# Fill constants of q and k written in eight transfers and later, large convolution constants loaded later, splits in another order

## The chip, the cores and the metric

The kernel runs on one core of a Trainium2 chip. What is measured is device time in microseconds from launch to the last output. A time is the median of several runs; a profile is one execution with the hardware's recorder on. The core has five engines with instruction streams of their own: TensorE (PE, matmuls, with its weight loads as PEld), VectorE (DVE), ScalarE (ACT), GpSimd (POOL) and SyncE (SP), which here issues nearly all transfers. Every engine works through its stream in order and stops at an instruction whose semaphores have not come yet. Sixteen DMA engines carry out the transfers.

## The reference

Two independent parts are computed and set side by side in the output. The first is attention over a window of 256 positions, with 32 heads of width 18, with its projections before and after. The second is a state-space convolution: a kernel K of length 2048 for each of 576 channels, computed from A, B, C and dt, and applied to u by a Fourier transform of twice the length.

```python
def _A_ref(x, wqkv, wo):                 # x [1, 2048, 576]
    qkv = (x @ wqkv).reshape(B, S, 3, H, Dh).transpose(2, 0, 3, 1, 4)
    q, k, v = qkv[0], qkv[1], qkv[2]     # H = 32, Dh = 18
    scores = jnp.einsum("bhqd,bhkd->bhqk", q, k) * (Dh ** -0.5)
    mask = (idx[:, None] - idx[None, :] >= 0) & (idx[:, None] - idx[None, :] < 256)
    p = softmax(jnp.where(mask, scores, -1e9))
    return (p @ v).transpose(0, 2, 1, 3).reshape(B, S, D) @ wo

def _B_ref(u, A_re, A_im, B_re, B_im, C_re, C_im, log_dt, Dskip):
    dt = jnp.exp(log_dt)[:, None]        # D = 576 channels, N = 128 states
    P = jnp.exp((dt * A)[:, :, None] * l[None, None, :])
    K = jnp.einsum("dn,dnl,dn->dl", Cc, P, dt * Bc).real
    y = irfft(rfft(pad(u)) * rfft(pad(K)))[:L]
    return y + u * Dskip

return jnp.concatenate([a, b], axis=-1)
```

## The kernel before

The two parts are cut into small steps and woven into one another. Each kind of step is a stream, written as a generator: the projection of q, k and v (`proj`), the tables of exponentials and sines of the convolution (`g_fac` to `g_taps`), the scores and their maxima (`smax`, `scores`), the products with v (`pv`), the transforms of the convolution (`cload`, `cspec`, `cinv`, `hload`, `clast`) and some more. Nothing is scheduled by the machine: four strings (`PLAN`) name one after the other the stream that takes its next step, for the parts "front", "tables", "first" and "rest". A digit behind a letter takes the oldest posted follow-up of that stream, such as the copy out of PSUM or the store of what was copied. So the order of instructions on each engine, and of transfers on SP, is the order of the strings.

SP's transfers go through one hardware queue, and each waits until the eighth transfer before it has landed. So at most eight are in flight, and they share the DMA engines in the order of their issue.

The projection works through the 2048 tokens in four quarters c (512 tokens each). For each quarter x is split into a high and a low 16-bit half (`xconv`, lines 376 to 387): ACT makes the high half `xh`, for each half h of the quarter; DVE makes the rest `xl` of rows 0 to 511 (line 384, long) and a low half of the last 64 rows, which goes into the fifth block of `xh` (line 386, short). Each product on PE then is a sum of fourteen matmuls (line 205), whose fifth reads that block. Nine products give q and k; ACT (line 451) and DVE (line 454) copy their high and low halves to a tile `qst` (three buffers), and SP stores them (lines 467 and 468) to the DRAM arrays `qz` and `kz`, of shape [4 quarters, 8 groups, 64 rows, 4, 512] in 16 bits. Four more give v, for which ACT's copies (line 443) go to four tiles `vst0` to `vst3` and SP's stores to `vd` (line 472). The first quarter's v is made apart, by `vfirst`.

Rows 0 to 53 of `qz` and `kz` are what is stored; rows 54 to 63 are constant, -32768. They are written from a constant tile `ones` in two transfers at the end of `vfirst` (lines 412 to 414), one for `qz`, one for `kz`, in the front. Row 54 is overwritten later in SBUF with the maxima of the scores (`raw<-m`, line 935, four small transfers for each of the 16 items of attention). An item is one quarter of the queries with eight heads; its q, k and v are loaded by `parts` (lines 880 to 884).

Meanwhile the tables of the convolution's kernel are made (lines 506 to 660): taps go from PSUM to a tile `kst` (line 649 on DVE, two buffers) and with two transfers to `gk` (line 641). Tiles `ust` with the first transform of u go to `gx` (line 496). In the part "rest", `conv_load` loads from both an `xk` of each of 24 steps (line 708), `spectra` (line 720) multiplies it with the constants `w2`, and `inverse` (line 754) the product with `i1`. Both constants, [128, 8, 256] in 32 bits, and a small one `i2` are loaded by `conv_setup` at the start of this part (line 778). The constants of the masks and maxima (`idb`, `sm`, `tm`, `idf`) are loaded by `early` (line 840).

Of the kernel before, what the change touches and what calls it, by code (L numbers as in the profile page):

```python
# [11 lines left out]
F16 = mybir.dt.float16  # L12
# [3 lines left out]
OP = mybir.AluOpType  # L16
# [5 lines left out]
CQ = 512  # L22
# [20 lines left out]
def constants():  # L43
# [23 lines left out]
    for nm, v in mult.items():  # L67
# [16 lines left out]

PLAN = {
    "front":
        "AAACVAAAVCAAAVAAV1V1VCACVVV1AAAAVCAV1VCVV1CVCCCCAPV1CVCBBCBVACAV1V1VVCPCBPPPP1CP2P4PPPP1CP2P4PBCBPPP"
        "1P",
    "tables":
        "GG1GG5PG6GP1P2P2GPG5G6GG2NG1G2G5G6GPPPPPP4P4G5G6P1P2MM1P4MMM1MNP1GG1RP2PNPPPP4RRG2GGP1GG5P2PG6G5G6NG"  # L90
        "1MM1XX1NRG2RPMUUU1U2UUUU2XMRPM1U1MP1P2PP4X1PXX5GGG5X2G6P1MG5RRG6PXX1XGM1MNX1MRG1G2M1NP2PPXX2PPU4X5RR"
# [64 lines left out]
class Kernel:  # L156
# [219 lines left out]
    def xconv(self, c):  # L376
        nc = self.nc
        self.xh = xh = self.p["xx"].tile([128, 5, 512], F16, name="xh")
        self.xl = xl = self.p["xx"].tile([128, 4, 512], F16, name="xl")
        for hf in range(2):  # L380
            t = self.xt[2 * c + hf]
            h = xh[:, :, hf * 256:hf * 256 + 256]
            nc.scalar.activation(h, t, AF.Copy, scale=self.sx)
            nc.vector.scalar_tensor_tensor(xl[:, :, hf * 256:hf * 256 + 256], t[:, 0:4], self.sx, h[:, 0:4],
                                           op0=OP.mult, op1=OP.subtract)
            nc.vector.scalar_tensor_tensor(h[64:128, 4], t[64:128, 4], self.sx[64:128], h[64:128, 4],
                                           op0=OP.mult, op1=OP.subtract)

    def vfirst(self):
        nc, w = self.nc, self.wt  # L390
        for tk in range(4):
            v, x = self.vst[tk], self.xt[tk // 2]
            ts = slice(tk % 2 * 128, tk % 2 * 128 + 128)
            ps = []
            for hf in range(2):
                yield "PE", (w, x), "pp"
                ps.append(self.p["pp"].tile([128, 512], F32, name="pp")[:, :288])
                for k in range(4):
                    nc.tensor.matmul(ps[hf], x[:, k, ts], w[:, k, 1152 + 288 * hf:1440 + 288 * hf],
                                     start=(k == 0), stop=False)  # L400
            yield "PE", ()
            for hf in range(2):
                r = slice(64 * hf, 64 * hf + 64)
                nc.tensor.matmul(ps[hf], x[r, 4, ts], w[r, 4, 1152 + 288 * hf:1440 + 288 * hf], start=False, stop=True)
            for hf in range(2):
                self.post("1", (ps[hf],), lambda v=v, hf=hf, x=ps[hf]: nc.scalar.activation(  # L406
                    v[:, 16 * hf:16 * hf + 16, 0:18], x.rearrange("p (h d) -> p h d", d=18), AF.Copy))
        yield "SP", (), lambda: self.known and not self.pend.get("V1")
        for tk in range(4):
            self.v_store(0, tk, self.vst[tk])  # L410
        yield "SP", ()
        for z in (self.qz, self.kz):
            nc.sync.dma_start(z[:, :, 54:64].rearrange("c g r p n -> (c g) r (p n)"),
                              self.ones[0:32].unsqueeze(1).to_broadcast([32, 10, 4 * CQ]))

    def proj(self):
        nc, w = self.nc, (self.wh, self.wl)
# [24 lines left out]
    def v_evac(self, c, tk, v, hf, x):  # L442
        self.nc.scalar.activation(v[:, 16 * hf:16 * hf + 16, 0:18], x.rearrange("p (h d) -> p h d", d=18), AF.Copy,
                                  scale=self.vsc)
        if hf:
            self.post("6", (v,), lambda: self.v_store(c, tk, v))

    def qk_hi(self, c, m, ps):
        nc, S = self.nc, 2.0 ** -24
# [253 lines left out]
    def conv_load(self, n):  # L703
        nc, fs, (ch, t) = self.nc, self.p["fs"], divmod(n, 8)
        x = self.cl[n] = fs.tile([128, 4, 2, 192], F32, name="xk")
        for m, g in enumerate((self.gx, self.gk)):
            yield "SP", ()
            nc.sync.dma_start(x[:, :, m], g[8 * t:8 * t + 8, :, :, 192 * ch:192 * ch + 192]
                              .rearrange("(s r) a l j -> (r a l) s j", r=2))

    def spectra(self, n):
        nc, tt, fy, t = self.nc, self.nc.vector.tensor_tensor, self.p["fy"], n % 8
# [58 lines left out]
    def conv_setup(self):  # L771
        nc, a, cc = self.nc, self.a, self.p["cc"]
        self.cl, self.Y, self.hp = {}, {}, {}
        self.i2 = cc.tile([128, 64], F32, name="i2")
        self.w2 = cc.tile([128, 8, 256], F32, name="w2")
        self.i1 = cc.tile([128, 8, 256], F32, name="i1")
        for n in ("w2", "i1", "i2"):
            nc.sync.dma_start(getattr(self, n), a["c_" + n])

    def cload(self):  # L780
        for n in range(24):
# [50 lines left out]
    def early(self):  # L832
        nc, a, ap = self.nc, self.a, self.p["const"]
        yield "SP", ()
        self.idb = ap.tile([128, 64], BF, name="idb")
        self.sm = ap.tile([128, 128], BF, name="sm")
        self.tm = ap.tile([128, 640], BF, name="tm")
        self.idf = ap.tile([128, 128], F32, name="idf")
        for t, n in ((self.idb, "c_id"), (self.sm, "c_sm"), (self.tm, "c_tm"), (self.idf, "c_if")):
            nc.sync.dma_start(t, a[n])  # L840
        for i in range(2):
            yield "SP", ()
            raw = {z: self.p["rawp"].tile([128, 5, 256], F32, name="raw").rearrange("p a b -> p (a b)") for z in "QKV"}
            q, k = (raw[z].bitcast(F16)[:, 0:4 * CQ].rearrange("p (a n) -> p a n", a=4) for z in "QK")
            self.sets[i].update({"Q": q, "V": raw["V"][:, 0:928]})
            self.first[i].update({"Q": q, "V": raw["V"][:, 0:928], "K": Shifted(k, 256), "k": k, "old": raw["K"]})
            nc.gpsimd.memset(raw["V"][:, 912:928], 0.0)
            for n, part in enumerate(self.parts(i)):
                if n:
                    yield "SP", ()  # L850
                part()
# [301 lines left out]
    def build(self):  # L1153
        nc, a = self.nc, self.a
        with ExitStack() as es:
# [28 lines left out]
            self.wh = self.p["wq"].tile([128, 5, 1728], F16, name="wh")  # L1184
            self.wl = self.p["wq"].tile([128, 5, 1728], F16, name="wl")
            self.vst = [self.p["pj"].tile([128, 32, 19], F32, name="vst%d" % i) for i in range(4)]
            self.ones = self.p["wrp"].tile([128, 4 * CQ], F16, name="ones")
            nc.gpsimd.memset(self.ones, -32768.0)
            self.known, self.conv_n = False, 0
            self.xh = self.xl = None  # L1190
# [84 lines left out]
```

## Time and profile before

| | |
|---|---|
| Median of 3 runs | 777.15 us (776.16 to 780.92) |
| The profiled execution's own time | 772.85 us |
| Its span | 771.1 us |
| Mean granted clock of PE | 0.98 |
| The two fills of `qz` and `kz` | 1280 KB each |
| Loads of `w2` and of `i1` | 1024 KB each |
| A store of `kst` | 256 KB |
| Bytes moved over the span | 150.67 MB, 195 GB/s in the mean |

The span is the time between the first and the last instruction that the recorder saw; the execution's own time is 1.75 us longer. The profiled execution was 4.3 us faster than the median. In all views, times count from the start of the span, and a name stands for all buffers of a tile: `w` is `w2`, `i` is `i1` or `i2`, `raw` is any buffer of a pool that serves in turn x, q, k and v.

### The profile page before, as it was taken

The page shows a single profiled execution, that of the slowest core. Times are in us where ns is not written, and L with a number is a line of the kernel's source. Part 1 is how long each engine was busy: PE and PEld are TensorE (multiplying, and loading weights), DVE is VectorE, ACT ScalarE, POOL GpSimd, SP SyncE. Part 2 cuts the span into 40 slices and gives each one's busy share as a digit, 9 for nine tenths or more (in the row PEclk, how much of TensorE's full clock was granted, in tenths as well). Part 3 has the DMA queues.
Part 4 walks back from the last instruction along what each step waited for, and adds up shares of the span by engine and source line. Part 5 has one row for each costly group of instructions (what it writes and reads, how often), then busy time and mean ns, then how long its engine had stood idle before and what let it go on. Part 6 is the DMA issues. An engine that isn't in the chain of part 4 may idle for free.

```text
span 771.1 us, 29480 instructions
## 1 busy us (share of the span) xinstructions
PE 686.8 (89%) x12956; PEld 403.5 (52%) x12956; DVE 538.7 (70%) x689; ACT 548.3 (71%) x755; POOL 415.8 (54%) x309
## 2 busy tenths in 40 slices
PE   3768768999999989999888998989899989999997
PEld 2523334556655655566445545545554545576675
DVE  5884888677787677888859877988886788631200
ACT  2267986888988878895467686677687687766722
POOL 2242886888788696867016553544255355354420
PEclk9978999999999999999989999999999999999999
DMA  8996342863657686757967667586588766767875
GB/s 308 345 248 151 86 109 56 196 156 97 133 146 201 145 195 188 178 150 155 244 213 236 201 186 246 176 273 183 177 246 233 231 206 191 230 189 250 251 237 174
DMA packets 215904, 150.67 MB, mean 195 GB/s; under 512 B 103530, under 2 KB 195818, under 8 KB 215520
## 3 DMA queue, kind: packets, MB, share of 16 engines
q1 hardware_dynamic: 214160, 146.28, 67.0%
q0 software_dynamic: 1616, 2.52, 1.1%
q8 instruction: 101, 1.65, 0.9%
q14 instruction: 27, 0.22, 0.1%
HBM read 83.50 MB, written 65.11 MB: 193 GB/s over the span
## 4 chain that ended last, share of the span: by engine, by line
PE 53%; DVE 12%; ACT 12%; issue 4%; DMA 4%; SPq 2%; POOL 0%; ACTq 0%; DVEq 0%
PE pp L205 9%; PE po L1022 9%; PE ring L205 7%; DVE m L942 5%; PE ring L908 4%; PE ring L754 4%; PE ring L984 4%; PE ring L720 3%; PE ring L617 2%; PE ring L817 2%; PE ring L494 2%; ACT P L1002 2%; PE ring L506 2%; DMA K<-kz 2%; PE ring L633 1%
## 5 line engine op out<-in xcount | busy, mean ns | idle before, releaser
L942 DVE TENSOR_REDUCE m<-ring 128x2 f32<-128x640 f32 (+4 forms) x256 | 188.3, 778 | 42.4 <-PE ring L916 37.1
L588 POOL TENSOR_TENSOR m<-A,tr 128x1024 f32<-128x1024 f32 x72 | 142.0, 1991 | 43.1 <-DVE m L594 37.1
L1002 ACT ACTIVATE P<-ring,esc 128x1024 f32<-128x1024 f32 (+2 forms) x86 | 88.4, 1060 | 28.7 <-PE ring L997 28.0
L1002 ACT ACTIVATE raw<-ring,esc 128x1024 f32<-128x1024 f32 (+2 forms) x74 | 76.9, 1061 | 28.6 <-PE ring L997 26.7
L736 POOL TENSOR_TENSOR t<-X 128x768 f32<-128x768 f32 x24 | 45.9, 1913 | 79.7 <-ACT X L728 79.5
L1065 POOL TENSOR_TENSOR oh<-osb,oh 128x1024 f16<-128x1024 f32 x16 | 35.4, 2211 | 66.2 <-ACT oh L1061 63.3
L205 PE MATMUL pp<-xh,wh 128*128 128x512 f16 x180 | 47.3, 393 | 14.5 <-ACT vst L406 6.4
L205 PEld LDWEIGHTS <-wh 128*128 128x128 f16 x324 | 31.2, 100 | 49.6 <-issue 10.5
L916 PE MATMUL ring<-sm,idb 64*64 64x128 bf16 x896 | 52.8, 219 | 0.0
L603 DVE TENSOR_TENSOR Q<-fr,ring 128x1024 f32<-128x1024 f32 x36 | 43.8, 1216 | 11.6 <-ACT ring L527 11.3
L728 ACT ACTIVATE X<-ring 128x768 f32<-128x768 f32 x48 | 36.7, 811 | 21.2 <-PE ring L720 12.5
L594 DVE TENSOR_TENSOR m<-m,m 128x1024 f32<-128x1024 f32 x36 | 48.3, 1342 | 4.2 <-POOL m L588 4.2
L1057 POOL TENSOR_TENSOR osb<-osb,T 128x1024 f32<-128x1024 f32 x16 | 37.8, 2365 | 24.3 <-DVE T L1052 21.8
L205 PE MATMUL pp<-xh,wl 128*128 128x512 f16 x180 | 48.5, 403 | 1.5 <-DVE wl L373 1.5
L908 PE MATMUL ring<-K,raw 54*64 54x320 f16 (+4 forms) x576 | 43.3, 308 | 5.6 <-DVE m L942 1.6
L569 POOL TENSOR_TENSOR tr<-tr,mab 128x768 f32<-128x768 f32 x18 | 33.7, 1871 | 25.6 <-ACT tr L564 25.6
L908 PEld LDWEIGHTS <-raw 54*64 54x64 f16 x704 | 26.1, 104 | 39.3 <-issue 35.6
L742 POOL TENSOR_TENSOR Y<-t,t 128x384 f32<-128x384 f32 x24 | 24.0, 1000 | 39.7 <-DVE t L736 18.7
L720 PE MATMUL ring<-xk,w 64*32 64x384 f32 x768 | 41.5, 491 | 3.5 <-issue 2.8
L997 PE MATMUL ring<-tm,idb 64*64 64x256 bf16 (+2 forms) x640 | 44.6, 257 | 0.0
L984 PEld LDWEIGHTS <-K 55*64 55x64 f16 x1280 | 29.1, 106 | 27.8 <-issue 24.0
L617 PE MATMUL ring<-Q,m 128*32 128x64 f32 x2304 | 39.2, 220 | 4.1 <-DVE m L594 2.0
(170 smaller groups left out, 1668.5 us busy)
## 6 DMA issues: line engine op xcount, KB each, us to landing
gx<-ust SPq DMA_DIRECT2D x16, 576.0 KB
gk<-kst SPq DMA_DIRECT2D x36, 256.0 KB
xk<-gx SPq DMA_DIRECT2D x24, 384.0 KB
xk<-gk SPq DMA_DIRECT2D x24, 384.0 KB
h<-ho SPq DMA_DIRECT2D x48, 192.0 KB
hp<-h SPq DMA_DIRECT2D x24, 384.0 KB
K<-kz SPq DMA_DIRECT2D x14, 512.0 KB
raw<-qz SPq DMA_DIRECT2D x11, 512.0 KB
```

The lines of the kernel that those rows point to most:

```text
L205: self.nc.tensor.matmul(ps, u, v, start=(i == 0), stop=(i == len(ops) - 1))
L588: tt(m[part], A[:, ch, a0:a0 + 8].unsqueeze(3).to_broadcast(sh), tr[:, ch, part, 0:8].unsqueeze(2).to_broadcast(sh), op=OP.mult)
L594: self.nc.vector.tensor_tensor(m[0], m[0], m[1], op=OP.add)
L617: nc.tensor.matmul(kp[32 * st:32 * st + 32, j, :], m[:, ch, 32 * term:32 * term + 32], Q[:, ch, term, :], start=(term == 0), stop=(term == ...
L720: nc.tensor.matmul(pi[i][32 * b:32 * b + 32, s, :384], self.w2[64 * r:64 * r + 64, t, o:o + 32], x[64 * r:64 * r + 64, 2 * s + q].rearrang ...
L736: mul(ts[i], X[:, :, :, :192].rearrange("p i s j -> p s i j"), X[:, i, :, 192:].unsqueeze(2).to_broadcast(sh), op=OP.mult)
L908: nc.tensor.matmul(ps[z:z + 64, b, :n], d["Q"][rr, 2 * b + pp, 64 * qb:64 * qb + 64], d["K"][rr, 2 * b + pp, k0:k1], start=True, stop=Fals ...
L916: nc.tensor.matmul(out, self.idb[rr], self.sm[rr], start=False, stop=True, skip_group_check=True)
L942: self.nc.vector.tensor_reduce(out, x, axis=AX.X, op=OP.max)
L984: nc.tensor.matmul(ps[z:z + 64, b, off:off + w], d["K"][rr, 2 * b + pp, kc:kc + 64], d["Q"][rr, 2 * b + pp, q0:q0 + w], start=(k == 0), st ...
L1002: nc.scalar.activation(P[:, :, lo:hi], ps[:, :, lo:hi], AF.Exp, scale=self.esc)
L1022: nc.tensor.matmul(po[32 * p:32 * p + 32, z, q0:q0 + w], V[64 * z:64 * z + 64, kb * 76 + 19 * p:kb * 76 + 19 * p + 32], P[p % 2][64 * z:64 ...
```

## The change

It has three parts, and the string "front" loses one letter.

First, the fills. The two large transfers at the front go. A new function `fill(z)` writes the constant rows of one quarter of `qz` or `kz`, 320 KB in a transfer of shape 8 x 80 x 256, from the first 8 partitions of `ones`, which now holds 256 values in each of 32 partitions in place of 2048. For the quarters 1 to 3, `qz` is filled behind the store of the first tile of v, `kz` behind that of the second; for quarter 0 both stand in `early`, behind the four constants.

Second, `xconv`. For the quarters 1 to 3 DVE makes both short low halves first and then both long ones.

Third, `conv_setup` loads only `i2`; `w2` is loaded behind the first `xk<-gx` and `i1` behind the first `xk<-gk`.

```diff
     def xconv(self, c):
-        for hf in range(2):
-            t = self.xt[2 * c + hf]
-            h = xh[:, :, hf * 256:hf * 256 + 256]
+        hs = [(self.xt[2 * c + hf], *(z[:, :, hf * 256:hf * 256 + 256] for z in (xh, xl))) for hf in range(2)]
+        for t, h, _ in hs:
             nc.scalar.activation(h, t, AF.Copy, scale=self.sx)
-            nc.vector.scalar_tensor_tensor(xl[:, :, hf * 256:hf * 256 + 256], t[:, 0:4], self.sx, h[:, 0:4],
-                                           op0=OP.mult, op1=OP.subtract)
+
+        def low(t, h, _):
             nc.vector.scalar_tensor_tensor(h[64:128, 4], t[64:128, 4], self.sx[64:128], h[64:128, 4],
                                            op0=OP.mult, op1=OP.subtract)
+
+        def rest(t, h, l):
+            nc.vector.scalar_tensor_tensor(l, t[:, 0:4], self.sx, h[:, 0:4], op0=OP.mult, op1=OP.subtract)
+
+        a, b = hs
+        for f, x in ((low, a), (low, b), (rest, a), (rest, b)) if c else ((rest, a), (low, a), (rest, b), (low, b)):
+            f(*x)
 
     def vfirst(self):
...
-        yield "SP", ()
-        for z in (self.qz, self.kz):
-            nc.sync.dma_start(z[:, :, 54:64].rearrange("c g r p n -> (c g) r (p n)"),
-                              self.ones[0:32].unsqueeze(1).to_broadcast([32, 10, 4 * CQ]))
+
+    def fill(self, z):
+        z = z[:, 54:64].rearrange("g r p n -> g (r p n)").rearrange("g (y x) -> g y x", x=256)
+        self.nc.sync.dma_start(z, self.ones[0:8].unsqueeze(1).to_broadcast([8, 80, 256]))
...
     def v_evac(self, c, tk, v, hf, x):
...
+        def store():
+            self.v_store(c, tk, v)
+            if tk < 2:
+                self.fill((self.qz, self.kz)[tk][c])
+
         if hf:
-            self.post("6", (v,), lambda: self.v_store(c, tk, v))
+            self.post("6", (v,), store)
...
     def conv_load(self, n):
...
+            if n == 0:
+                z = ("w2", "i1")[m]
+                nc.sync.dma_start(getattr(self, z), self.a["c_" + z])
...
     def conv_setup(self):
...
-        for n in ("w2", "i1", "i2"):
-            nc.sync.dma_start(getattr(self, n), a["c_" + n])
+        nc.sync.dma_start(self.i2, a["c_i2"])
...
     def early(self):
...
+        for z in (self.qz, self.kz):
+            self.fill(z[0])
...
     def build(self):
...
-            self.ones = self.p["wrp"].tile([128, 4 * CQ], F16, name="ones")
+            self.ones = self.p["const"].tile([32, 256], F16, name="ones")
             nc.gpsimd.memset(self.ones, -32768.0)
```

In the listings of the order below, a row is a line of the kernel, the operation, output and input with their buffer numbers, and the shape; x2 is two in a row. The numbers of lines and buffers shift a little between the two kernels.

SP's transfers around the first place of the new fills, where the stores of v's second quarter end and the constants of the masks follow, before:

```order
L472 DMA vd_74<-vst0_147 64x8x76 x2
L472 DMA vd_74<-vst1_148 64x8x76 x2
L840 DMA idb_2149<-in_c_id_dram 128x64
L840 DMA sm_2150<-in_c_sm_dram 128x128
L840 DMA tm_2151<-in_c_tm_dram 128x640
L840 DMA idf_2152<-in_c_if_dram 128x128
L641 DMA gk_70<-kst_1794 128x16x32 x2
L641 DMA gk_70<-kst_2077 128x16x32 x2
```

The same place after:

```order
L483 DMA vd_74<-vst0_147 64x8x76 x2
L420 DMA qz_72<-ones_151 8x80x256
L483 DMA vd_74<-vst1_148 64x8x76 x2
L420 DMA kz_73<-ones_151 8x80x256
L853 DMA idb_2149<-in_c_id_dram 128x64
L853 DMA sm_2150<-in_c_sm_dram 128x128
L853 DMA tm_2151<-in_c_tm_dram 128x640
L853 DMA idf_2152<-in_c_if_dram 128x128
L420 DMA qz_72<-ones_151 8x80x256
L420 DMA kz_73<-ones_151 8x80x256
L652 DMA gk_70<-kst_1792 128x16x32 x2
L652 DMA gk_70<-kst_2077 128x16x32 x2
```

Four fills stand ahead of the taps' stores; the third quarter has its two between stores of v in the same way (further back on SP), and the fourth too.

SP's transfers at the start of the part "rest", where the large constants were loaded, before (`kst` and the maxima `m16` are stored, the rest is loaded):

```order
L641 DMA gk_70<-kst_4899 128x16x32 x2
L778 DMA w2_5264<-in_c_w2_dram 128x2048
L778 DMA i1_5265<-in_c_i1_dram 128x2048
L778 DMA i2_5263<-in_c_i2_dram 128x64
L935 DMA raw_3599<-m16_5101 1x16x64 x4
L880 DMA raw_2942<-qz_72 128x2048
L880 DMA K0_4730<-kz_73 128x4x512
L708 DMA xk_5269<-gx_69 128x4x192
L708 DMA xk_5269<-gk_70 128x4x192
```

The same place after:

```order
L652 DMA gk_70<-kst_4905 128x16x32 x2
L791 DMA i2_5269<-in_c_i2_dram 128x64
L950 DMA raw_3603<-m16_5107 1x16x64 x4
L895 DMA raw_2944<-qz_72 128x2048
L895 DMA K0_4736<-kz_73 128x4x512
L719 DMA xk_5273<-gx_69 128x4x192
L723 DMA w2_5270<-in_c_w2_dram 128x2048
L719 DMA xk_5273<-gk_70 128x4x192
L723 DMA i1_5271<-in_c_i1_dram 128x2048
```

The two large constants now stand behind the stores of the maxima and the loads of q and k.

DVE's operations on the second quarter of x, before:

```order
L515 TENSOR_TENSOR fr_847<-ring_836,fr_847 128x512
L384 SCALAR_TENSOR_TENSOR xl_856<-raw_123,xr_257,xh_855 128x4x256
L386 SCALAR_TENSOR_TENSOR xh_855<-raw_123,xr_257,xh_855 64x256
L384 SCALAR_TENSOR_TENSOR xl_856<-raw_125,xr_257,xh_855 128x4x256
L386 SCALAR_TENSOR_TENSOR xh_855<-raw_125,xr_257,xh_855 64x256
L603 TENSOR_TENSOR Q_936<-fr_639,ring_844 128x32x32
```

The same place after:

```order
L526 TENSOR_TENSOR fr_845<-ring_834,fr_845 128x512
L385 SCALAR_TENSOR_TENSOR xh_853<-raw_123,xr_257,xh_853 64x256
L385 SCALAR_TENSOR_TENSOR xh_853<-raw_125,xr_257,xh_853 64x256
L389 SCALAR_TENSOR_TENSOR xl_854<-raw_123,xr_257,xh_853 128x4x256
L389 SCALAR_TENSOR_TENSOR xl_854<-raw_125,xr_257,xh_853 128x4x256
L614 TENSOR_TENSOR Q_934<-fr_637,ring_842 128x32x32
```

The two short operations have moved ahead of the two long ones; what stands around them is as before.

More of the change, by code (lines that the diff above doesn't have):

```diff
@@ L86 @@
     "front":
-        "AAACVAAAVCAAAVAAV1V1VCACVVV1AAAAVCAV1VCVV1CVCCCCAPV1CVCBBCBVACAV1V1VVCPCBPPPP1CP2P4PPPP1CP2P4PBCBPPP"
-        "1P",
+        "AAACVAAAVCAAAVAAV1V1VCACVVV1AAAAVCAV1VCVV1CVCCCCAPV1CVCBBCBVACAV1V1VCPCBPPPP1CP2P4PPPP1CP2P4PBCBPPP1"
+        "P",
     "tables":
```

## The prediction

> **What bounds the kernel now.** I read the profile's page first: the span, the busy times and the engines of the chain that ended last.
>
> ```profile
> span 771.1 us, 29480 instructions
> PE 686.8 (89%) x12956; PEld 403.5 (52%) x12956; DVE 538.7 (70%) x689; ACT 548.3 (71%) x755; POOL 415.8 (54%) x309
> PE 53%; DVE 12%; ACT 12%; issue 4%; DMA 4%; SPq 2%; POOL 0%; ACTq 0%; DVEq 0%
> ```
>
> The tensor engine is busy for 89% and carries 53% of the chain; DMA and SP's queue carry 6%. No transfer bounds the kernel as a whole. But PE runs in order, so a DMA that comes late stops it, and the 84 us in which it is idle are all there is to win. I therefore went to the places that the change touches: the timelines of SP, ACT, PE and DVE there, and the busy time of the DMA engines in stretches around them. The columns of a timeline row are start, duration, engine, line, operation, output and input, count, and in brackets the idle time ahead of it with what ended it. The columns of a stretch are its ends and length, the busy time of PE, weight loads, DVE, ACT and POOL, PE's granted clock, the DMA share and GB/s.
>
> **The fills leave the front.** Two fills of 1280 KB are issued at 47.48 and 48.12; the stores of q behind them go out slowly, and ACT waits for one of them.
>
> ```profile
> 47.48 0.59 SPq L413 DMA_DIRECT2D qz<-ones  x1
> 48.12 0.58 SPq L413 DMA_DIRECT2D kz<-ones  x1
> 54.58 2.38 SPq L467 DMA_DIRECT2D qz<-qst  x1
> 57.01 2.46 SPq L468 DMA_DIRECT2D qz<-qst  x1
> 64.99 0.60 ACT L451 ACTIVATE qst<-pp 128x512 f16<-128x512 f32 x1 [3.47 <-DMA qz<-qst]
> 66.96 1.08 PE L506 MATMUL ring<-c_ct,Tim 96*128 96x512 bf16 x2 [2.83 <-DVE fr L515]
> 55.00:61.00 6.00, 6.00 (x31) 2.74 (x29) 4.98 (x4) 2.54 (x5) 2.73 (x1) 1.00 0.99 200
> ```
>
> A store takes SP some 2.4 us here, since each waits for the eighth DMA before it, and the engines are full (share 0.99) with the fills. ACT's 3.47 us become PE's 2.83 us two microseconds later. Without the fills the stores land as soon as they are issued. Gain: 2.8 (PE's wait) to 3.5 us (ACT's); I take 3.4, since the wait is ACT's and PE stands behind it. The shorter preset of the constant costs nothing: it is on POOL, ahead of all this.
>
> The last row also prices the new fills. The fills read 32 partitions, and the engines, all busy, move 200 GB/s. Stores that read all 128 partitions move nearly twice that with the same share:
>
> ```profile
> 283.00:284.00 1.00, 0.91 (x5) 0.43 (x5) 0.98 (x2) 0.77 (x3) 1.00 (x1) 1.00 1.03 376
> ```
>
> So the rate goes with the number of partitions that are read, or something that comes with it, more than with the engines. The new fill reads only partitions 0 to 7, for 320 KB. If a quarter of the partitions gives a quarter of the rate (50 GB/s), a fill takes 320 KB / 50 GB/s = T = 6.55 us, as long as an old one with four times the bytes. That is the upper end. The lower end is the old rate, 200 GB/s: T = 1.64. Between them lies a limit by the DMA engines alone: if the outer size of 8 lets only 8 of the 16 take part, each at an old fill's 12.5 GB/s, T = 3.3 us. I take 6.55, because 32 against 128 partitions already shows the rate falling with the partitions read, at a full share. The old row shows 32 partitions at half of the 376 GB/s, so a proportional fall below 32 is an estimate.
>
> [...]
>
> **Eight short fills at three places.** Four stand at 183 to 196 us (one behind each of two stores of v, two behind the constants of the maxima), two near 268 to 281, two near 348 to 356. All DMAs of SP pass through the same engines in order, so what is issued behind a fill lands T later. What counts is how long the engines idle there now, before the first instruction that waits.
>
> ```profile
> 183.28 5.71 SPq L472 DMA_DIRECT2D vd<-vst  x4
> 187.00:189.00 2.00, 2.00 (x15) 1.20 (x13) 2.00 (x3) 1.34 (x4) 1.26 (x1) 1.00 0.01 2
> 189.00:196.00 7.00, 6.31 (x116) 4.83 (x115) 6.64 (x8) 6.94 (x12) 5.36 (x3) 1.00 0.87 160
> 196.00:200.00 4.00, 3.49 (x28) 2.48 (x26) 3.18 (x5) 4.00 (x10) 2.44 (x2) 1.00 0.02 4
> 205.29 0.69 DVE L649 COPY kst<-ring 128x512 f32<-128x512 f32 x1
> 206.03 0.38 PE L506 MATMUL ring<-c_ct,Tim 96*128 96x512 bf16 x1 [0.28 <-DVE kst L649]
> ```
>
> Place 1: the copy at 205.29 needs the buffer whose two stores stand right behind the four fills. Now they are done at 196. The slack is 205.3 - 196 = 9.3 us, plus 2.0 + 0.13 x 7 = 2.9 us in which the engines idle before that, less an estimated 0.8 until the last store is seen: 11.4. The stall is 4T - 11.4 = 14.8 us at 6.55, 1.8 at 3.3, none at 1.64. Behind the copy stand the rest of DVE's program and, 0.05 us later, PE.
>
> ```profile
> 267.00:284.40 17.40, 15.81 (x176) 10.66 (x169) 10.06 (x12) 15.63 (x27) 15.60 (x14) 1.00 0.93 199
> 284.40:286.40 2.00, 1.57 (x7) 0.57 (x6) 1.94 (x3) 0.80 (x2) 1.91 (x3) 1.00 0.02 8
> 289.00:290.40 1.40, 1.40 (x7) 0.64 (x8) 1.40 (x2) 0.70 (x2) 1.29 (x1) 1.00 0.62 179
> 291.90 0.60 ACT L451 ACTIVATE qst<-pp 128x512 f16<-128x512 f32 x1 [0.34 <-PE pp L205]
> 345.00:358.00 13.00, 13.00 (x280) 9.24 (x278) 10.84 (x15) 7.45 (x14) 10.08 (x9) 1.00 0.93 188
> 358.00:361.00 3.00, 2.78 (x47) 2.05 (x48) 2.75 (x7) 1.00 (x2) 2.12 (x2) 1.00 0.09 13
> 356.59 2.74 SPq L935 DMA_DIRECT2D raw<-m  x4
> 364.00 0.42 PE L984 MATMUL ring<-raw 55*64 55x64 f16 x12
> 209.15 1.96 DMA qz<-qst
> ```
>
> Place 2: the engines idle 0.07 x 17.4 + 0.98 x 2.0 + 0.38 x 1.4 = 3.7 us before ACT's copy at 291.90, the first that needs a buffer of a store behind the fills; with 0.4 between 286.4 and 289 that is 4. Stall 2T - 4 = 9.1, 2.6 or none. Place 3: they idle 0.07 x 13 + 0.91 x 3 = 3.6 us until 361; the last store of maxima, issued at 359.33, lands near 361.3 by the chain's row, 2.7 before PE needs it at 364.00. The slack is between 3.6 and 6.3; I take 5.4, nearer the upper end, since these stores are small. Stall 2T - 5.4 = 7.7, 1.2 or none. Together 8T - 20.8 = 31.6 us at T = 6.55. SP's issue of a fill, 0.6 us as at 47.48, runs while the engines still move the one before; it adds nothing.
>
> **The splits in another order.** DVE's four operations are the same; the two short ones come first.
>
> ```profile
> 106.00 2.88 DVE L384 SCALAR_TENSOR_TENSOR xl<-raw,xr,xh 128x1024 f16<-128x1024 f32 x1
> 108.89 2.08 DVE L386 SCALAR_TENSOR_TENSOR xh<-raw,xr,xh 64x256 f16<-64x256 f32 x1
> 113.88 0.48 DVE L386 SCALAR_TENSOR_TENSOR xh<-raw,xr,xh 64x256 f16<-64x256 f32 x1
> 114.42 0.59 PE L205 MATMUL pp<-xh,wh 128*128 128x512 f16 x1 [4.32 <-DVE xh L386]
> 118.64 0.69 DVE L649 COPY kst<-ring 128x512 f32<-128x512 f32 x1 [0.76 <-PE ring L637]
> 120.60 1.10 PE L617 MATMUL ring<-Q,m 128*32 128x64 f32 x64
> 201.47 1.29 DVE L384 SCALAR_TENSOR_TENSOR xl<-raw,xr,xh 128x1024 f16<-128x1024 f32 x1 [0.56 <-ACT xh L383]
> ```
>
> In the second quarter of the tokens PE waits 4.32 us until both short ones are done, at 114.36. In the new order they are done after 106.0 + 2 x 2.1 = 110.2 at the latest, and PE's wait goes. But DVE still ends the four at 114.4, and until 120 it has only 0.76 us of idle time, ended by PE. PE's matmul at 120.60 reads a product that DVE makes after all this. So PE arrives there early and waits again: of 4.32 us about 0.5 stay (between none and 1.5; a loss of 0.8 if PE's earlier matmuls push DVE's order of waits). In the third quarter (201.47) and the fourth PE has other work; nothing.
>
> **The large constants.** Two transfers of 1024 KB stand ahead of four tiny stores of maxima.
>
> ```profile
> 376.17 2.12 SPq L778 DMA_DIRECT2D w<-in_c_w_dram  x1
> 379.39 7.95 DMA raw<-m
> 387.38 1.07 PE L984 MATMUL ring<-raw 55*64 55x64 f16 x12 [2.27 <-DMA raw<-m]
> 380.00:387.00 7.00, 4.74 (x128) 2.43 (x127) 6.17 (x10) 1.59 (x2) 0.00 (x0) 0.99 1.01 374
> 387.00:394.00 7.00, 6.27 (x111) 3.88 (x119) 2.40 (x4) 5.08 (x5) 0.00 (x0) 0.52 1.02 319
> 397.41 0.88 PE L720 MATMUL ring<-xk,w 64*32 64x384 f32 x16
> ```
>
> The second row is of the chain: the stores land 7.95 us after their issue, behind 2 MB; PE idles 2.26 of 7 us, and for the 7 us after that the granted clock is 0.52. Moved behind, the constants free the stores: 2.27 us of idle time, and up to 2 more if the clock stays up, since 6.27 us of matmuls at about half clock could take some 3. I take 4 (2.3 to 4.5). The cover: the first matmul that reads the weights is at 397.41. The queue has 2.9 MB to bring by then (q, k, x, weights), at 374 to 319 GB/s 8 to 9 us from 383: 392. It holds, by 5 us.
>
> **Sum.** 31.6 - 3.4 - 0.5 - 4.0 = +23.7 us. The profiled execution took 772.85 us, 4.3 under the median of the runs shown, so this gives 796.6 against the profile and 801 against the median; I say 798. In general the change is 8T - 28.7, zero at T = 3.6.
>
> **The rivals.** (a) The fills are limited by the number of DMA engines and not by the partitions: T = 3.3, stalls of 1.8 + 2.6 + 1.2 = 5.6 us, gains 7.9, -2.3 in all: 775 against the median, 771 against the profile; call it 773. [...] (b) The other side: the fills run at the old rate, T = 1.64. Then each fits into the idle time of its place (6.6 of 11.4, 3.3 of 4, 3.3 of 5.4 us) and only the gains are left: -7.9, 769. It decides as soon as T is below 2. For it: the places were idle by 2 to 12 us, and half of a fill's cost may be per DMA. Against it: 200 against 376 GB/s. (c) A part of the stalls is won back, as ACT and POOL run ahead while PE stands: if a third comes back, +13, 787. This lies inside my own case.
>
> **How the numbers follow.** The partition case with (c) in it has 0.70, its own range 784 to 808 (a third won back and a little more, to the upper bounds of the terms); (a) has 0.15, (b) 0.15. The predicted time is 798. The range of 8 in 10 reaches from 770, which takes in (a) and the upper half of (b), to 808. A measurement here tells about 1% (7.8 us) from no change: below 769.4, above 784.9. Slower by over 1% is my case less its low end, 0.66; within 1% is (a) and parts of both neighbours, 0.20; faster by over 1% is half of (b) and a little, 0.14.
>
> **What would show it.** If I am right, the stretches behind a fill have a DMA share near one (or half, for eight engines) at some 50 GB/s for 6 us, DVE's copy of the taps near 205 waits some 15 us for a store, ACT's copy of q near 290 waits for one, PE near 364 waits for the maxima. At the front the 3.47 us of ACT are gone, at 387 the 7.95 us of the chain and the low clock. I am wrong if the fills move over 100 GB/s, if those three waits are under 3 us together, or if the stores behind a fill overtake it on engines that it leaves free.

## The result, and the profile after

The changed kernel takes 812.55 us in the median (810.44 to 814.20, 4 runs) against 778.05 us before: 1.0439 times as long, with an interval of 1.0396 to 1.0481. The forecast was 798 with a range up to 808. The sign and the main cause were right. The amount was not: 34.5 us were lost, not the 23.7 of the sum.

The page of the changed kernel, its span, the busy times of the engines and the engines of the chain that ended last:

```profile
span 811.2 us, 29484 instructions
PE 697.6 (86%) x12956; PEld 408.0 (50%) x12956; DVE 539.1 (66%) x689; ACT 548.5 (68%) x755; POOL 411.3 (51%) x309
PE 51%; ACT 14%; DVE 12%; DMA 10%; SPq 6%; issue 5%; ACTq 0%; POOL 0%; DVEq 0%
```

DMA and SP's queue now have 16% of the chain where they had 6%. PE does the same 12956 matmuls, but at a mean granted clock of 0.956 in place of 0.98 it is busy for 10.8 us longer, and it is idle for 29 us longer (811.2 - 697.6 against 771.1 - 686.8). The profiled execution before was 5 us faster than its median, so the profiles differ by 40 us where the medians differ by 34.5.

The first place of the new fills, in the timelines of SP, DVE and PE, and the busy times in four stretches of 1 us (columns as in the prediction):

```profile
184.38 0.49 SPq L420 DMA_DIRECT2D qz<-ones  x1
201.82 18.78 SPq L652 DMA_DIRECT2D gk<-kst  x4
220.45 0.69 DVE L660 COPY kst<-ring 128x512 f32<-128x512 f32 x1 [13.30 <-DMA gk<-kst]
221.19 0.59 PE L517 MATMUL ring<-c_ct,Tim 96*128 96x512 bf16 x1 [15.72 <-DVE kst L660]
221.57 2.34 PE L205 MATMUL pp<-xh,wl 128*128 128x512 f16 x5
206.00:207.00 1.00, 0.00 (x0) 0.00 (x0) 1.00 (x1) 1.00 (x3) 1.00 (x2) 1.00 0.38 48
210.00:211.00 1.00, 0.00 (x0) 0.00 (x0) 0.00 (x0) 0.00 (x0) 0.87 (x1) 0.54 1.02 148
212.00:213.00 1.00, 0.00 (x0) 0.00 (x0) 0.00 (x0) 0.00 (x0) 0.00 (x0) 0.50 0.38 48
224.00:225.00 1.00, 1.00 (x4) 0.32 (x3) 0.00 (x0) 0.00 (x0) 0.00 (x0) 0.50 0.75 236
```

A fill that runs alone moves 48 GB/s with a DMA share of 0.38 (the rows at 206 and 212); the prediction would have had a share near one, or half. So 320 KB (327,680 bytes) take 6.8 us; the forecast had taken 6.55. The store of taps waits behind four fills, DVE's copy waits 13.3 us for it, and PE 15.7; some 2 us of PE's wait come of the splits, after which DVE is later at the copy (see e5_x_only). The row is the one that the prediction named, and the size is near (14.8). The last four rows show one thing more: PE's last matmul ends at 205.5, the granted clock is 0.54 from 210 to 211 and 0.50 at 212, and it is still 0.50 at 224, 3 us after PE has begun again, so five matmuls take 2.34 us (1.24 at full clock, as e6_warm shows).

The other two places, in the timelines of ACT and PE:

```profile
302.76 0.64 ACT L510 COPY ust<-ring 128x576 f32<-128x576 f32 x1 [3.63 <-DMA gx<-ust]
318.81 0.60 ACT L462 ACTIVATE qst<-pp 128x512 f16<-128x512 f32 x1 [4.82 <-DMA kz<-qst]
401.07 1.22 PE L999 MATMUL ring<-raw 55*64 55x64 f16 x12 [7.87 <-DMA raw<-m]
```

At the second place two waits of ACT share the delay, 8.45 us together against 9.1 forecast; the earlier one, for a store of the first transform of u, was not named. At the third, PE waits 7.87 us for the maxima (7.7). At the front and at the start of the last part the timeline of ACT, the chain and the timeline of PE show:

```profile
61.81 0.62 ACT L462 ACTIVATE qst<-pp 128x512 f16<-128x512 f32 x1
424.13 9.94 DMA xk<-gk
434.21 2.81 PE L734 MATMUL ring<-xk,w 64*32 64x384 f32 x32 [0.95 <-DMA xk<-gk]
430.00:434.00 4.00, 2.89 (x73) 1.26 (x73) 2.79 (x6) 1.37 (x2) 0.00 (x0) 0.74 1.03 399
```

ACT no longer waits for a store of q at the front, and it starts there 3.2 us earlier. The transfer on the chain at the late constants is no longer the store of maxima. It is the load of x behind the first constant, with 9.94 us from issue to use, and PE waits there 0.95 us in its turn while its granted clock falls (0.74 in the mean from 430 to 434).

### The profile page after: what moved, and what is told of

It reads as the page before. It is cut to its first block, busy times and chain, and to the rows that moved or that the text cites. A ratio compares the mean times of both kernels' runs of the same rounds, so it can differ in the third digit from the quotient of the medians.

```text
span 811.2 us, 29484 instructions
## 1 busy us (share of the span) xinstructions
PE 697.6 (86%) x12956; PEld 408.0 (50%) x12956; DVE 539.1 (66%) x689; ACT 548.5 (68%) x755; POOL 411.3 (51%) x309
## 4 chain that ended last, share of the span: by engine, by line
PE 51%; ACT 14%; DVE 12%; DMA 10%; SPq 6%; issue 5%; ACTq 0%; POOL 0%; DVEq 0%
PE pp L205 9%; PE po L1037 8%; PE ring L205 7%; PE ring L923 4%; DVE m L957 4%; PE ring L768 4%; PE ring L734 4%; PE ring L999 4%; PE ring L517 2%; DMA gx<-ust 2%; PE ring L830 2%; DMA wraw<-in_wr_dram 2%; DVE amx L193 2%; ACT P L1017 2%; PE ring L505 2%
## 5 line engine op out<-in xcount | busy, mean ns | idle before, releaser
L205 PE MATMUL pp<-xh,wh 128*128 128x512 f16 x180 | 51.0, 418 | 9.9 <-ACT vst L412 7.1
```

The source lines that it names most:

```text
L205: self.nc.tensor.matmul(ps, u, v, start=(i == 0), stop=(i == len(ops) - 1))
```

## The experiments

Every ratio is against the kernel before in the same batch of runs, with its 95% interval; it need not equal the quotient of two medians. "Half clock" means a granted clock of 0.50 in the rows.

**Which partitions are read (e1_step4).**

```diff
-        self.nc.sync.dma_start(z, self.ones[0:8].unsqueeze(1).to_broadcast([8, 80, 256]))
+        self.nc.sync.dma_start(z, self.ones[0:32:4].unsqueeze(1).to_broadcast([8, 80, 256]))
```

> The changed kernel with one edit: the fills read partitions 0, 4, 8 ... 28 of the constant in place of 0 to 7. Bytes, shape, number of transfers and their places are the same. If the rate hangs on which partitions are read, a fill takes 3.3 us or less in place of some 6.8, the waits of PE near 205 to 221 and near 400 all but go, and the time is 772 to 780. If eight engines or 512-byte rows set the rate, a fill still takes some 6.8 us at 48 GB/s and the time stays at 810 to 815.

777.2 us, 1.0028 [1.0005, 1.0050]. One slice of eight partitions is worth 1.0439 - 1.0028 = 4.1%, or 32 us. In this kernel a fill alone shows, in a stretch of 0.5 us:

```profile
189.50:190.00 0.50, 0.50 (x6) 0.40 (x5) 0.50 (x2) 0.50 (x3) 0.50 (x1) 1.00 0.58 175
```

175 GB/s in place of 48, with the same bytes, the same outer size of 8, the same rows of 512 bytes and the same places. A fill takes 1.9 us, and no engine waits any more for a store behind a fill at the three places. So the choice of the eight partitions set the rate of 48 GB/s, and neither the outer size nor the short rows did.

**Other distances (e8_step16).**

```diff
-        self.nc.sync.dma_start(z, self.ones[0:8].unsqueeze(1).to_broadcast([8, 80, 256]))
+        self.nc.sync.dma_start(z, self.ones[0:128:16].unsqueeze(1).to_broadcast([8, 80, 256]))
-            self.ones = self.p["const"].tile([32, 256], F16, name="ones")
+            self.ones = self.p["const"].tile([128, 256], F16, name="ones")
```

> The changed kernel, but the fills read partitions 0, 16, 32 ... 112. [...]

786.45 us, 1.0125 [1.0069, 1.0181]: in between, though the partitions are farther apart than in e1_step4. A stretch behind a fill, and PE's wait at the first place, of which 2.33 us stand in e1_step4 too:

```profile
189.00:190.00 1.00, 1.00 (x8) 0.55 (x6) 1.00 (x2) 0.34 (x2) 0.75 (x1) 1.00 0.41 84
211.61 0.59 PE L517 MATMUL ring<-c_ct,Tim 96*128 96x512 bf16 x1 [4.39 <-DVE kst L660]
```

Distance as such doesn't help: the closer set, 0, 4 ... 28, gave 175 GB/s and 1.9 us a fill, and 0, 16 ... 112 some 80 GB/s (74 to 84 where a fill runs alone). What in the pattern sets the rate was not shown. At 80 GB/s a fill takes T = 4.1 us, and the prediction's formulas give 4T - 11.4 = 5.0, 2T - 4 = 4.2 and 2T - 5.4 = 2.8, or 12 us; measured over e1_step4 are 0.97%, or 7.5. The waits for the three stores are 1.98 us of DVE, 3.71 of ACT and 1.7 of PE, together 7.4.

**The parts alone (e3_fills_only, e2_oldfills, e4_w2_only).** Each is the kernel before or the changed one with whole hunks of the change taken or undone; shown are the lines that matter:

```diff
 # e3: the kernel before with
+            if tk < 2:
+                self.fill((self.qz, self.kz)[tk][c])
...
 # e2: the changed kernel with
-                self.fill((self.qz, self.kz)[tk][c])
+        for z in (self.qz, self.kz):
+            nc.sync.dma_start(z[:, :, 54:64].rearrange("c g r p n -> (c g) r (p n)"),
+                              self.ones[0:32].unsqueeze(1).to_broadcast([32, 10, 4 * CQ]))
...
 # e4: the kernel before with
+            if n == 0:
+                z = ("w2", "i1")[m]
+                nc.sync.dma_start(getattr(self, z), self.a["c_" + z])
```

> The kernel before with only the eight new fills in place of the two large ones. If the fills are the cause, the time is that of the changed kernel, 810 to 816, with PE's wait of about 15 us near 205 and of about 8 us near 400. If the parts work together, it is under 805.

807.02 us, 1.0413 [1.0366, 1.0460]. The fills alone bring the loss, within the intervals.

> The changed kernel with the two large fills put back at the front; the order of the splits and the late constants stay. If the fills are all of the loss, the time is that of the kernel before or under it. By the prediction's terms (0.5 and 4.0 us) it is 773.5. If the late constants give back what they win, as the new wait for x at 434 us in the changed kernel suggests, it is 776 to 780. Over 785 would mean that one of these two parts is also to blame.

779.22 us, 1.0050 [1.0025, 1.0076]. Without the new fills the other two parts are no gain but a small loss: not 4.5 us faster, but 3.9 slower.

> The kernel before with only the two large constants of the convolution loaded later. By the prediction's term it is 4 us faster (774). If the load of x behind them is late in turn and PE's clock falls there instead of at 387, it is within 1.5 us of before.

774.26 us, 0.9992 [0.9961, 1.0024]: nothing, as the rival said. In the chain of this kernel the store of maxima has left, and the first row has come; the second is from PE's timeline:

```profile
388.21 9.38 DMA xk<-gk
397.73 2.80 PE L726 MATMUL ring<-xk,w 64*32 64x384 f32 x32 [0.18 <-DMA xk<-gk]
```

The four small stores no longer wait behind 2 MB, and the load of x that the spectra need now stands behind 1 MB. But PE waits only 0.18 us for it. The two timelines of PE show where the gain goes. At 380 PE is 3.1 us behind the kernel before (380.73 against 377.60, the scores' first matmuls). At the products near 393 it is 1.1 ahead (392.82 against 393.95), so 4.2 us are won, near the 4.0 of the forecast. When the spectra begin it is 0.3 behind again (397.73 against 397.41), and their first 32 matmuls take 2.80 us in place of 1.52. So 2.7 of the 4.2 us are lost by their end.

**One constant alone (e11_i1_only).**

```diff
+            if n == 0 and m:
+                nc.sync.dma_start(self.i1, self.a["c_i1"])
-        for n in ("w2", "i1", "i2"):
+        for n in ("w2", "i2"):
```

> The kernel before with only the constant of the inverse transform loaded later, that of the spectra at its old place. If the late constants give back their gain because the spectra's constant stands ahead of the load of x for which PE then waits, half of the gain is won here without that wait: 1 to 3 us faster than before. If the gain is lost elsewhere, it is within 1 us of before.

775.35 us, 1.0006 [0.9978, 1.0035]. Nothing again, so the theory of the load of x is a miss. Here no transfer is on the chain from 370 to 450, and PE does not wait for x ahead of the spectra. Still the same happens: PE wins 4.2 us up to the products near 393 (from 1.0 behind the kernel before to 3.2 ahead, 390.77 against 393.95) and loses 2.7 by the end of the first spectra, whose 32 matmuls take 2.81 us here:

```profile
395.59 2.81 PE L725 MATMUL ring<-xk,w 64*32 64x384 f32 x32
```

Ahead of them PE waits once for 1.2 us (0.94 in e4_w2_only) for nothing that the profile shows. What that is stays open.

**The splits alone (e5_x_only), and in the second quarter alone (e9_x_second).** The lines are those of e9, against the line of the change, which e5 has as it is.

```diff
-        for f, x in ((low, a), (low, b), (rest, a), (rest, b)) if c else ((rest, a), (low, a), (rest, b), (low, b)):
+        for f, x in ((low, a), (low, b), (rest, a), (rest, b)) if c == 1 else ((rest, a), (low, a), (rest, b), (low, b)):
```

> The kernel before with only the other order of the splits (both short ones first in quarters 1 to 3). By the prediction's term it is 0.5 us faster than before. The rival: in the third quarter DVE now waits for ACT's second copy before it may start a long split, ends the four some 2 us later (in the other runs with this order 6.0 us after ACT's first copy in place of 3.8), and hands that on, so the time is 2 to 4 us over before.

781.08 us, 1.0060 [1.0033, 1.0087]. The order that was costed as a gain of 0.5 us loses 4.7.

> The kernel before with the other order of the splits in the second quarter alone. If the loss of that order comes from the third quarter, where DVE stands between ACT's two copies, it is gone here and the time is within 1.5 us of before. If it comes from the second quarter, the time stays some 4 us over before.

779.08 us, 1.0057 [1.0030, 1.0085]: the same loss within the intervals. So the second quarter alone brings a loss, and the rival of e5 can't be all of it. It is not refuted, however: the difference of the two ratios is known to some 3 us only, and the trace of e5_x_only shows what the rival said. DVE ends the splits of the third quarter some 2 us later, and PE waits for the copy behind them 2.33 us, in place of 0.28 before and in e9_x_second:

```profile
210.88 0.38 PE L515 MATMUL ring<-c_ct,Tim 96*128 96x512 bf16 x1 [2.33 <-DVE kst L658]
```

e1_step4 has the same wait, and PE stays that much later until 380. In the second quarter DVE needs 8.1 us for the four (8.4 before). The timelines of PE and DVE of e9_x_second there, and a stretch:

```profile
111.29 0.38 PE L205 MATMUL pp<-xh,wh 128*128 128x512 f16 x1 [0.24 <-DVE xh L385]
117.71 2.12 PE L642 MATMUL ring<-Kq,wk 32*128 32x256 f32 x14 [4.96 <-DVE Q L615]
120.53 0.69 DVE L658 COPY kst<-ring 128x512 f32<-128x512 f32 x1 [1.81 <-PE ring L646]
116.00:120.00 4.00, 2.29 (x20) 2.12 (x22) 2.72 (x5) 1.49 (x4) 0.00 (x0) 0.50 0.05 16
```

Before, PE waited 4.32 us for the short split, and the six matmuls that it then did at half clock (0.50 from 114 to 117) were in nobody's way, because the next ones had to wait for DVE anyway (e13_before_warm below shows that wait). Now the six are done early, and PE waits in front of the matmuls that DVE waits for. These run at half clock (2.12 us for fourteen; 1.18 before), so DVE's copy comes 1 us later, and a second stretch of low clock follows near 133 to 136 (0.60 in the mean from 132 to 136; 1.00 before). In one kernel with the old order, e4_w2_only, the half clock behind this wait lasted until 124 (0.51 in the mean from 120), and it hit the same matmuls:

```profile
120.00:124.00 4.00, 4.00 (x23) 1.30 (x25) 4.00 (x5) 0.29 (x1) 2.19 (x2) 0.51 0.07 23
```

So the old order can lose here too. From PE's projection matmul at 109.07 in the kernel before to the one at 160.10, e4_w2_only falls 3.0 us behind the kernel before, the other kernels with the old order (e3, e7, e10, e11) some 0.5 at most. Of the seven with the new order six fall 3.0 to 3.5 us behind, and e8_step16, where the second stretch does not come, 1.2.

**That wait filled (e12_x_second_warm, e13_before_warm).** Matmuls with zero weights, which add zeros to the sum, stand in PE's wait:

```diff
+            self.zero = self.p["const"].tile([128, 128], F16, name="zero")
+            nc.gpsimd.memset(self.zero, 0.0)
...
                     self.mm14(ps, w, x, slice(m * 128, m * 128 + 128), slice(0, 512), part=part)
+                    if (c, m, part) == (1, 0, 1):
+                        for _ in range(20):
+                            nc.tensor.matmul(ps, self.zero, x[0][:, 0, :], start=False, stop=False)
```

> The kernel with the new order of the splits in the second quarter alone, and 20 matmuls of 128x512 with zero weights added to the sum that stands ahead of PE's wait of 4.96 us near 113 to 118; they add zeros. If the loss of that order (0.6%) is that PE idles in one piece, falls to half clock and then does at half clock the matmuls that DVE waits for, the wait is filled, the two stretches at half clock near 115 to 123 and 132 to 137 go, and the time is that of the kernel before or up to 2 us under it. If the loss has another cause, it stays some 4 us over before.

776.17 us, 0.9987 [0.9953, 1.0021]. Twenty useless matmuls take away the 0.6%, within the intervals. The timeline of PE and the same stretch, from an execution of 781.53 us, longer than the median by 5, which is read for this place alone:

```profile
113.89 4.48 PE L437 MATMUL pp<-xh,zero 128*128 128x512 f16 x20
119.02 1.38 PE L645 MATMUL ring<-Kq,wk 32*128 32x256 f32 x14 [0.65 <-DVE Q L618]
116.00:120.00 4.00, 3.35 (x23) 1.68 (x25) 4.00 (x6) 2.88 (x6) 0.00 (x0) 1.00 0.00 0
```

The clock stays at 1.00, and the fourteen take 1.38 us. Between the two matmuls named above PE loses 1.1 us, in place of 3.3 in e9_x_second. The stretch near 132 stayed (0.57 in the mean from 132 to 136), though it was expected to go.

> The kernel before with 18 such matmuls ahead of the fifth matmul of that sum, in PE's wait of 4.32 us near 110 to 114. If the half clock near 113 to 118 comes of this wait, it goes and the time is 1 to 3 us under before; if not, the stretch stays and the time is that of before.

777.14 us, 1.0014 [0.9980, 1.0048]. In the kernel before, the stretch at half clock went (1.00 from 108 to 136), but the gain of 1 to 3 us did not come: PE now waits in front of the next matmuls instead.

```profile
117.09 1.39 PE L636 MATMUL ring<-Kq,wk 32*128 32x256 f32 x14 [0.99 <-DVE Q L609]
```

**The stalls filled (e6_warm).**

```diff
+                        if c == 2 and m == 0:
+                            for _ in range(64):
+                                nc.tensor.matmul(ps, w[0][:, 0, 0:128], x[0][:, 0, :], start=True, stop=True)
```

The 30 at the third place stand ahead of the first scores in the same way.

> The changed kernel with matmuls added whose results are overwritten: 64 of 128x512 ahead of the one product that PE does before its wait near 205, and 30 of 54x512 ahead of the scores that wait near 393. They fill idle time and wait for nothing new. If the idle PE is what halves the clock, the waits end when they did (near 221 and 401), the stretches at half clock behind both go, and the time is some 6 us under the changed kernel (1.036 to 1.04 of before). If the low clock comes of something else, both stretches stay and the time is that of the changed kernel.

815.58 us, 1.0481 [1.0414, 1.0548]: not the 6 us faster that were expected, and not told apart from the changed kernel (1.0439). The timeline of PE and two rows of its waits:

```profile
205.92 13.99 PE L436 MATMUL pp<-xh,wh 128*128 128x512 f16 x64
222.49 0.38 PE L520 MATMUL ring<-c_ct,Tim 96*128 96x512 bf16 x1 [1.50 <-DVE kst L663]
222.71 1.24 PE L205 MATMUL pp<-xh,wl 128*128 128x512 f16 x5
PE po L1044 <- issue: 6.1, 7, 1.4
PE ring L631 <- issue: 4.1, 1, 4.1
```

The local half of the expectation held. PE's wait ended when it did, the stretches of half clock behind both stalls were gone (9 tenths or more in the page's slices from 204 to 225 and from 388 to 409 us, where the changed kernel's page has 6 and 8), and five matmuls took 1.24 us in place of 2.34. But this program waits longer for nothing that the profile shows ("issue"; the first of these two groups stood at 2.0 us in the changed kernel, the second at none). What that is stays open, and so is whether it comes in most executions: the profiled one took 819.36 us, two others 811. So this run doesn't say what the half clock behind the stalls costs as a whole.

**What is left without the losses (e7_fill4_only, e10_fill4_w2, e14_fill4_w2_warm).** The kernel before with the fills read from partitions 0, 4 ... 28, then also with the late constants, and then also with 18 matmuls of zero weights in PE's wait of 4.32 us, ahead of the fifth matmul of the second quarter's first sum:

```diff
 # e7: e3 with
+        self.nc.sync.dma_start(z, self.ones[0:32:4].unsqueeze(1).to_broadcast([8, 80, 256]))
 # e10: e7 and e4 together; e14: e10 with, ahead of the fifth matmul of that sum
+            for _ in range(warm if i == 4 else 0):
+                self.nc.tensor.matmul(ps[0:16], self.zero, xh[:, 0, :], start=False, stop=False)
```

> The kernel before with only the fills changed, and these read partitions 0, 4 ... 28 (a fill then takes some 1.9 us, 173 GB/s). By the prediction's terms 3.4 us are won at the front and every place has slack for its fills, so the time is 3.4 us under before. If what is won at the front is lost before 200 us, as the shifts of the other runs suggest, it is within 1.5 us of before.

776.82 us, 1.0003 [0.9974, 1.0032]. The 3.4 us of the front don't show. In this run ACT has no wait for a store at the front, but PE waited 2.41 us for DVE before 55.90 and then ran at a clock of 0.57 from 57 to 61, and ACT waited for PE:

```profile
60.81 0.60 ACT L456 ACTIVATE qst<-pp 128x512 f16<-128x512 f32 x1 [3.92 <-PE pp L205]
57.00:61.00 4.00, 4.00 (x12) 1.49 (x11) 3.92 (x4) 0.19 (x1) 0.00 (x0) 0.57 0.41 116
```

The profiles of e1_step4 and e8_step16 have the same stretch, behind the same wait (2.50 and 2.60 us). Those of the changed kernel, e3, e6, e10 and e14 do not; there the wait is 1.5 to 2.1 us, and at 80 PE is 1.8 to 3.2 us ahead of the kernel before.

> The changed kernel with the fills read from partitions 0, 4 ... 28 and with the splits in their old order: the fills moved and the constants late, without what the other runs showed to cost. By the prediction's terms for the front and the constants it is 7 us faster than before; by the runs of each alone (no gain in either) it is within 2 us of before.

772.28 us, 0.9973 [0.9943, 1.0003]. It is the lowest ratio of all kernels tried, 0.047 under that of the changed one. Against the kernel before its interval just reaches 1.

> The fills read from partitions 0, 4 ... 28, the constants late, the splits in their old order, and 18 matmuls with 16 columns of zero weights in the same wait. If both help, it is 3 to 6 us under before; if only the first does, some 2 us (as without them).

775.69 us, 1.0010 [0.9977, 1.0043]: no further gain.

## Why the prediction was right or wrong

| Step of the sum | Forecast, us | Measured, us | From |
|---|---|---|---|
| Stalls at the three places | +31.6 | +32 (waits alone 29.6) | changed kernel less e1_step4, 4.1%; 13.30 + 8.45 + 7.87 |
| Front | -3.4 | 0 (-2.0 to +2.5) | e7_fill4_only |
| Order of the splits | -0.5 | +4.7 (2.6 to 6.8) | e5_x_only |
| Large constants | -4.0 | -0.6 (-3.0 to +1.9) | e4_w2_only |
| Sum | +23.7 | +36 | the whole: +34.5 |

The fills and their stalls were right in cause and place, and near in size. The rate was taken to fall with the number of partitions read. For partitions 0 to 7 the forecast rate came (48 GB/s; 50 forecast), but their number doesn't set it: eight others gave 175 in e1_step4. Each stall was computed as the added transfer time less the idle time of the DMA engines. That the sum meets the measured 32 us so closely is in part luck. With the measured T of 6.83 us the formulas give 33.8, the three waits make 29.6, and the half clock behind them (0.50 at 224 in the changed kernel), which the sum left out, is in the 32 as well. How much it adds is open. Of the rivals, (a), the engine count, was an assumption that no run shows; e1_step4 excludes it with 175 GB/s at an unchanged outer size; (b), the old rate, by the changed kernel's own 48 GB/s; and of (c), a third won back, the medians show nothing.

The rest of the miss, some 11 us, is in the three gains, none of which came.

The step that failed most is the order of the splits, 5.2 us off. The prediction said that PE "arrives there early and waits again", which is what happened, and that "of 4.32 us about 0.5 stay", with a loss of at most 0.8. A reordering that only moves a wait was costed by the wait alone. What stands behind the wait counts too: PE's clock is at half when the wait ends (0.50 from 114 to 117 in the kernel before, from 116 to 120 in e9_x_second), and the new order put the matmuls that DVE waits for at that point. e9_x_second shows a loss there, and e12_x_second_warm its cause by filling the wait. Two more pairs of kernels that differ by the splits give the same size: e1_step4 less e10_fill4_w2 is 0.55%, e2_oldfills less e4_w2_only 0.58%. For the third quarter the prediction put "nothing", since PE has other work. But DVE has not: there its four splits take 6.0 us in place of 3.8, 0.77 of it a wait for ACT's second copy, and PE waits 2.05 us longer for the copy behind them (2.33 less 0.28). The medians can't tell how much of these 2 us is left at the end.

The large constants: the gain of 4 us was right, and it came (4.2 us near 393 in e4_w2_only and e11_i1_only), but the prediction ended its sum there. By the end of the first spectra 2.7 us of it are gone in both: PE idles ahead of them (0.94 and 1.2 us) and then takes 2.8 us in place of 1.52 for their first 32 matmuls. "The cover ... holds, by 5 us" was wrong too, since the load of x behind the first constant becomes the chain's transfer (9 to 10 us from issue to use). But PE waits for it only 0.18 us in e4_w2_only and not at all in e11_i1_only, so this is not the main part of the give-back. Why PE idles there stays open.

The front: ACT's wait went as forecast, and in the changed kernel it starts 3.2 us earlier there. SP's 2.4 us for a store were not a wait for the eighth transfer before, as the prediction has it: SP's waits in the kernel before from 46 to 63 us are for DVE and ACT (3.0 us the longest), none for a transfer. Why an issue takes that long there stays open. But the median of e7_fill4_only shows no gain. In its profile a clock of 0.57 behind another wait, of 2.41 us, took the time at 57 to 61. Three of the eight profiles of kernels with the new fills have that stretch; how often it comes over all runs is open.

## What to carry to other kernels

Before a transfer is cut into parts, look at which partitions each part reads: a quarter of the bytes from a quarter of the partitions took as long as the whole (6.8 us, 6.55 by the old fill's rate), and a stride in one slice was worth 32 us. The price of a late transfer was reckoned here as its own time times the number of transfers ahead of the waiting one, less the idle time of the DMA engines at that place; windows on the DMA share give that, and the sum came out within the interval here, for 48 as for 175 GB/s; for some 80 it was too high (12 us for 7.5). Where a reordering moves a wait on TensorE, look at what stands right behind the wait: if another engine waits for those matmuls, it can pay for a low clock as well (here fourteen of them took 2.12 us in place of 1.18). And a gain at one wait is not a gain at the end: follow PE's rows in both traces past it until the difference stays.

## What the runs showed of the hardware

Eight partitions as the source of a transfer gave 48, some 80 and 175 GB/s, for 0 to 7, for every sixteenth and for every fourth. The DMA engines show shares of 0.38 at 48 GB/s, 0.41 at 84 and 0.58 at 175.

PE's granted clock fell in or behind stretches in which PE idled. In the changed kernel PE's last matmul ahead of the first stall ends at 205.5; the clock was 1.00 until 210, 0.50 from 211 to 227 and 1.00 from 228, 7 us after PE's first matmul at 221.19. At the third place, where PE waited 7.87 us until 401.07, it was 0.50 from 398 to 408. In the kernel before, where PE waited 4.32 us until 114.42, it was 0.50 from 114 to 117 and 1.00 from 118. It was also low with 2.41 us of waiting in e7_fill4_only (0.57 from 57 to 61), and in the kernel before with 2.26 us of idle time out of 7 (0.52 from 387 to 394). Such stretches don't all lie at the same places from profile to profile: the kernel before has 1.00 from 57 to 61, e9_x_second 0.60 from 132 to 136 where the kernel before has 1.00. Single runs of the kernel before lie between 768 and 784 us, with mean clocks of 0.969 to 0.985; those with the lower clock tend to be the longer ones (correlation -0.5 to -0.7 in the four batches). The best kernel, e10_fill4_w2, has a mean clock of 0.988 in its profile; the changed one has 0.956.
